# One core, attention followed by a GLU and a bilinear layer: where q and k are split, how v is padded, and who adds a head's two parts

## The chip, the cores and the metric

The kernel runs on one NeuronCore of a Trainium2 chip. A core has five engines that run side by side, each with an in-order queue: TensorE (PE, and PEld for its weight loads), VectorE (DVE), ScalarE (ACT), GpSimd (POOL) and SyncE (SP), which here only issues DMAs. The metric is the device time of one launch in microseconds (us). Three runs of the kernel before took 1189.56 to 1189.74 us, median 1189.6 us.

## The reference

```python
scores = q @ k.T / 8                       # 4 batches x 8 heads, 576 tokens, head_dim 64
scores = where(scores >= scores.max(-1) - tau, scores, -1e9)
attn   = exp(scores - scores.max(-1)); attn /= attn.sum(-1) + 1e-9
x      = (attn @ v)  as [2304 tokens, 512]
x      = (silu(x @ w_gate) * (x @ w_val)) @ w_out        # 512 -> 1536 -> 512
out    = ((x @ w1) * (x @ w2) @ w3) @ w_out2             # 512 -> 1024 -> 512
```

The weights arrive as 64-bit floats and have to be turned into 32-bit ones on the chip.

## The kernel before, in words

Every matmul operand is kept as two parts, `hi` (rounded to the format in which TensorE is fast) and `lo` (what is left), and products are made in three or four passes from these parts.

**Attention.** Work goes by *pairs* of heads, p = 0 to 15, four pairs to a batch. A pair has nine score *tiles* (i = 0 to 8; i = 4 is that of the last 64 queries of both heads, the "left" queries). A tile is scored on TensorE into `s_bank` (`mm_scores`), reduced to its row maximum by VectorE (`el_max`, L482), exponentiated by ScalarE (`el_exp`, L491), masked and summed by VectorE two tiles later (`el_mask`, L501), which needs the threshold that GpSimd adds (`el_thr`, L474, tile `stat`). Two queues of further items are worked off between the tiles by credits (`some`): `main` (transposes of the masked tiles, `it_T` and others, whose `hi` and `lo` go to `AT`, `ATL` through one of three paths X, Y, Z, and the products with v, `it_pv`) and `prep` (the next pair's operands). In path Y the `lo` half is GpSimd's (L100, L103), from a copy of the bank in a `tmp` or `raw` buffer.

`prep` has five items for the next pair: `it_k` and `it_q` transpose k and q into a bank of `t_bank` and copy `hi` out (L340); `it_k2` and `it_q2` subtract `hi` in the bank by a matmul with minus the identity (`less`, L335), copy `lo` out (L345), and issue the twelve DMAs that stack `hi` and `lo` into the operands `L` and `R` (`stack`, L348, L349); `it_left` does the same for the left queries. Prep earns 0.8 credits in a tile.

The v of the last 64 keys has to be padded with zeros to stand in a 128-row operand, `VLZ`. `split_left` splits it for a whole batch into `vls`; `split_v` copies it into `VLZ` for each pair with two DMAs (L309). In the product with v the `hi` part of v gives rows 0 to 63 of `xs` and its `lo` part rows 64 to 127. Both parts are stored separately in DRAM, `x_dram[2, ...]`, with two DMAs for each head (L599).

**GLU and bilinear layer.** The tokens go in five blocks. `x_prep(j, kk)` loads both parts of a piece of x and the reciprocal sums into two 4 KB slots (L790, L795), GpSimd adds the parts (L826), VectorE multiplies (L829), ScalarE and VectorE split the result (L817, L818). Weights are loaded and converted a *unit* at a time: `conv_step` finishes one unit (L157, then L196 on ScalarE and L199 on GpSimd or VectorE) and starts the next (`conv_bits`: L139, L142, L145 on VectorE, L148 and L149 on ScalarE, L150 on GpSimd). The items of `early()` come into `prep` when the last pair starts: three `conv_step` and the four `x_prep` of block 0. Then the GLU begins, `glu_step`, with the matmuls of `mm3` (L835).

The order on each engine is made at build time by a list scheduler that respects the data and the buffers: it may hoist instructions, and what it chose is shown below where it matters.

Of the kernel before, what the change touches and what calls it, by code (L numbers as in the profile page):

```python
# [34 lines left out]
def kernel(  # L35
# [171 lines left out]

    def conv_step(n=1):

        old = []  # L210
        while conv_mid and conv_mid[0][2]() and len(old) < n:
            old.append(conv_mid.popleft())
            old[-1][1](conv_value(old[-1][0]))
# [14 lines left out]
    def attention(actx, early, tail):  # L228
# [8 lines left out]
        ta = lctx.enter_context(tc.tile_pool(name="ta", bufs=N_TA))  # L237
        raw_i, in_tail = [0], []

        def raw_tile():  # L240
            raw_i[0] += 1
            if in_tail or raw_i[0] % (N_TA + N_TMP) >= N_TA:
                return tmp()
            return ta.tile([P, 512], F32, tag="raw", name="raw")

# [105 lines left out]
        halves = {}  # L351

        def it_q(p):
            hi = sp.tile([P, 512], F32R, tag="qhi", name="qhi")
            halves[p, 0] = (turn(raws.pop((p, 0)), hi, 0.125), hi)

        def it_k(p):
            hi = sp.tile([P, 512], F32R, tag="khi", name="khi")
            halves[p, 1] = (turn(raws.pop((p, 1)), hi, 1.0), hi)

        def it_q2(p):
            L, R = qk_tiles(p)
            bank, hi = halves.pop((p, 0))
            lo = sp.tile([P, 512], F32R, tag="qlo", name="qlo")
            turn_lo(bank, hi, lo, 0.125)
            stack(L[:, 0, :], lo, hi, 0)
            stack(L[:, 1, :], hi, lo, 1)
            stack(L[:, 2, :], hi, lo, 0)
            stack(L[:, 3, :], lo, hi, 1)

        def it_k2(p):
            L, R = qk_tiles(p)
            bank, hi = halves.pop((p, 1))
# [759 lines left out]
```

## Time and profile before

| | |
|---|---|
| median of three runs | 1189.6 us |
| the profiled execution | 1189.26 us, of which the span from first to last instruction is 1187.3 us |
| attention, roughly | 0 to 365 us |
| GLU, its weights' conversion included | 358 to 810 us |
| conversion and product of w3 and the second w_out | 810 to 890 us |
| bilinear layer | 890 us to the end |

Busy time is what an engine's instructions cover. TensorE's clock is given as a granted share: 1.00 is 2.4 GHz and 0.50 is 1.2 GHz. A bracket behind a row of the timeline is the idle time before it and what ended that.

### The profile page before, as it was taken

How to read it: one execution, taken by the hardware profiler on the slowest of the kernel's cores; microseconds unless marked ns; L12 is line 12 of the kernel's file. 1: busy time of each engine (PE TensorE's matmuls, PEld its weight loads, DVE VectorE, ACT ScalarE, POOL GpSimd, SP SyncE). 2: the span in 40 equal slices, each digit the busy share in tenths (PEclk: the TensorE clock that was granted, in tenths of full speed). 3: DMA queues.
4: the chain of work that ended last, by engine and by line, in shares of the span. 5: the costliest groups of instructions: out<-in, count | busy, mean ns of one | idle time of the engine just before them, and what ended most of it. 6: DMA issues, size and time to landing. Idle time of an engine off the chain costs nothing.

```text
span 1187.3 us, 16882 instructions
## 1 busy us (share of the span) xinstructions
PE 1122.1 (95%) x6074; PEld 959.8 (81%) x6074; DVE 733.1 (62%) x1272; ACT 590.3 (50%) x1071; POOL 475.7 (40%) x457
## 2 busy tenths in 40 slices
PE   7898998899878999999999999999899999999998
PEld 6788888788766777888888888888787888888886
DVE  7987868778798797656464664567892022432222
ACT  6877878778786456443242432345563231321111
POOL 4575665565663655443232332234241221321110
PEclk9999999999989999999999999999999999999999
DMA  8865756656455743222111120123430010100024
GB/s 197 224 146 141 163 132 142 146 121 142 107 170 167 216 126 100 75 68 71 31 59 36 37 89 8 47 93 103 124 107 18 1 36 1 37 1 1 1 58 102
DMA packets 107891, 108.14 MB, mean 91 GB/s; under 512 B 48800, under 2 KB 82208, under 8 KB 107808
## 3 DMA queue, kind: packets, MB, share of 16 engines
q1 hardware_dynamic: 107808, 107.06, 34.3%
q8 instruction: 48, 0.79, 0.3%
q14 instruction: 35, 0.29, 0.1%
HBM read 68.16 MB, written 14.23 MB: 69 GB/s over the span
## 4 chain that ended last, share of the span: by engine, by line
PE 55%; DVE 5%; DMA 2%; ACT 1%; issue 1%; POOL 0%; POOLq 0%; DVEq 0%; ACTq 0%
PE t_bank L835 36%; PE s_bank L835 19%; DMA raw<-in_moe_w_dram 2%; DVE tmp L157 1%; DVE slot L818 1%; DVE raw L142 1%; DVE tmp L145 1%; DVE tmp L139 0%; DVE slot L911 0%; PE t_bank L908 0%; DVE slot L199 0%; DVE slot L1022 0%; DVE slot L882 0%; DVE slot L1059 0%; ACT raw L148 0%
## 5 line engine op out<-in xcount | busy, mean ns | idle before, releaser
L835 PE MATMUL t_bank<-slot,slot 128*128 128x512 f32 (+1 forms) x2592 | 559.7, 371 | 5.9 <-DVE slot L818 2.4
L835 PEld LDWEIGHTS t_bank<-slot,slot 128*128 128x128 f32 x2592 | 457.0, 189 | 92.8 <-DVE slot L818 3.3
L835 PE MATMUL s_bank<-h,slot 128*128 128x512 f32 (+1 forms) x720 | 161.9, 372 | 3.4 <-ACT slot L884 2.2
L150 POOL TENSOR_TENSOR raw<-raw 128x512 int32<-128x512 int32 x76 | 84.4, 1111 | 182.1 <-ACT raw L149 171.6
L501 DVE SCALAR_TENSOR_TENSOR P<-P,stat,E 128x576 f32<-128x576 f32 x144 | 148.3, 1043 | 5.6 <-POOL stat L474 3.9
L835 PEld LDWEIGHTS s_bank<-h,slot 128*128 128x128 f32 x720 | 126.8, 190 | 27.1 <-ACT slot L884 2.6
L482 DVE TENSOR_SCALAR_CACHE_REDUCE P<-s_bank,neg 128x576 f32<-128x576 f32 x144 | 114.2, 809 | 55.2 <-PE s_bank L443 55.2
L1069 DVE TENSOR_TENSOR tmp<-tmp,t_bank 128x512 f32<-128x512 f32 (+1 forms) x40 | 25.3, 633 | 178.2 <-PE t_bank L835 178.2
L107 POOL TENSOR_TENSOR h<-tmp,h 128x512 fp32r<-128x512 f32 (+1 forms) x60 | 74.4, 1239 | 136.1 <-ACT h L106 136.0
L1073 POOL TENSOR_TENSOR h<-tmp,h 128x512 fp32r<-128x512 f32 (+1 forms) x38 | 45.8, 1205 | 200.5 <-ACT h L1071 200.5
L491 ACT ACTIVATE E<-P,stat 128x576 f32<-128x576 f32 x144 | 116.4, 812 | 9.7 <-DVE P L482 8.8
L443 PE MATMUL s_bank<-R,L 128*128 128x288 f32 x512 | 101.2, 318 | 14.7 <-DVE P L482 5.6
L920 DVE TENSOR_TENSOR tmp<-tmp,t_bank 128x512 f32<-128x512 f32 (+1 forms) x60 | 37.9, 631 | 113.1 <-PE t_bank L835 104.5
L835 PE MATMUL s_bank<-slot,h 128*128 128x512 f32 x432 | 106.6, 391 | 0.9 <-DVE slot L1059 0.8
L328 PE MATMUL t_bank<-ident,P 128*128 128x128 f32 x640 | 90.5, 277 | 14.5 <-DVE AT L524 4.7
L443 PEld LDWEIGHTS s_bank<-R,L 128*128 128x128 f32 x512 | 76.8, 194 | 26.7 <-DVE P L482 15.1
L835 PEld LDWEIGHTS s_bank<-slot,h 128*128 128x128 f32 x432 | 79.9, 188 | 18.3 <-DVE slot L1059 2.1
L882 DVE TENSOR_TENSOR slot<-s_bank,slot 128x1024 f32<-128x1024 f32 (+1 forms) x72 | 82.2, 1146 | 18.5 <-PE s_bank L835 16.5
L328 PEld LDWEIGHTS t_bank<-ident,P 128*128 128x128 f32 x640 | 74.2, 141 | 23.5 <-DVE ATL L524 4.6
L583 PE MATMUL t_bank<-AT,sp 128*128 128x288 f32 x512 | 87.5, 307 | 5.3 <-DVE AT L524 2.4
L157 DVE SCALAR_TENSOR_TENSOR tmp<-tmp,raw 128x512 f32<-128x512 f32 x76 | 72.0, 948 | 30.5 <-POOL raw L150 30.5
L919 ACT ACTIVATE tmp<-t_bank 128x512 f32<-128x512 f32 (+1 forms) x60 | 33.2, 554 | 113.3 <-PE t_bank L835 106.9
(110 smaller groups left out, 1427.9 us busy)
## 6 DMA issues: line engine op xcount, KB each, us to landing
raw<-in_moe_w_dram SPq DMA_DIRECT2D x32, 512.0 KB, 3.8
raw<-in_moe_w_out_dram SPq DMA_DIRECT2D x20, 512.0 KB, 3.5
x_dram<-xs SPq DMA_DIRECT2D x64, 144.0 KB, 2.4
L<-qhi SPq DMA_DIRECT2D x60, 128.0 KB, 2.9
L<-qlo SPq DMA_DIRECT2D x60, 128.0 KB, 2.5
raw<-in_moe_w_gate_dram SPq DMA_DIRECT2D x12, 512.0 KB, 3.7
raw<-in_moe_w_val_dram SPq DMA_DIRECT2D x12, 512.0 KB, 3.8
ld<-in_k_dram SPq DMA_DIRECT2D x16, 256.0 KB, 4.0
```

What stands on the lines that cost most here:

```text
L107: nc.gpsimd.tensor_tensor(out=lo, in0=src, in1=f32(hi), op=ALU.subtract)
L150: nc.gpsimd.tensor_tensor(out=a, in0=a, in1=x, op=ALU.subtract)
L157: nc.vector.scalar_tensor_tensor(out=f32(m), in0=f32(m), scalar=2.0 ** 20, in1=f32(a), op0=ALU.add, op1=ALU.mult)
L328: nc.tensor.matmul(bank[:, t * P:(t + 1) * P], lhsT=part, rhs=ident, is_transpose=True, start=(t == 0), stop=(t == len(parts) - 1),)
L443: nc.tensor.matmul(o, lhsT=lhs, rhs=R[:, c:c + HALF], start=(h == hs2[0] and e == 0), stop=(h == hs2[-1] and e == 1),)
L482: nc.vector.tensor_scalar(out=p_tile(p, i).rearrange("p (a c) -> p a c", a=2), in0=sb[:, :, 0:HALF], scalar1=neg, scalar2=None, op0=ALU.mu ...
L491: nc.scalar.activation(out=e, in_=p_tile(p, i), func=ACTF.Exp, scale=-1.0, bias=stats[p // HP][:, 0, c:c + 1],)
L501: nc.vector.scalar_tensor_tensor(out=t, in0=t, scalar=stats[b][:, 1, c:c + 1], in1=e, op0=ALU.is_le, op1=ALU.mult, accum_out=sums[b][:, c: ...
L583: nc.tensor.matmul(o, lhsT=vs[:, 4 * h + c, :, :].rearrange("p a d -> p (a d)"), rhs=AT[h][:, e, c, cs], start=(c == 0 and e == 0), stop=F ...
L835: nc.tensor.matmul(o, lhsT=lhs(a), rhs=rhs(c), start=(first and i == 0), stop=(last and i == 2))
L882: nc.vector.tensor_tensor(out=a, in0=s, in1=a, op=ALU.add)
L1073: (nc.vector if end else nc.gpsimd).tensor_tensor(out=h[:, 1, 0:n], in0=ab[:, 0:n], in1=f32(h[:, 0, 0:n]), op=ALU.subtract)
```

## The change

Four edits, and some sizes that follow from them.

1. `it_k2` and `it_q2` go. `turn` puts the second half (the matmul with minus the identity, the copy of `lo`, the stacking DMAs) into the list `deferred`, whose entries run behind the next item. Prep has three items for a pair and earns 1.0 credit in a tile.
2. `split_left` writes `VLZ` itself, for all four pairs of a batch, with GpSimd instructions on 64 partitions; two such tiles alternate by batch. The two DMAs of each pair go.
3. Three weight units are converted inside attention, one each in pairs 3, 6 and 9 (from tile 4 on); `early()` only issues loads and the four `x_prep`.
4. GpSimd issues a DMA that adds `xs[64:128]` onto `xs[0:64]`, and SP stores the sum alone. `x_dram` has one part, `x_prep` needs one slot and one load in place of two parts, and GpSimd's addition goes.

The seventh buffer for copies of path Y (`raw`) goes as well, and the slot pools change from 7 and 8 to 6 and 9.

```diff
-N_U1, N_U2, N_U3, N_U4 = 3, 7, 8, 24
-N_TMP, N_BIG, N_HB, N_TA = 6, 3, 3, 1
+N_U1, N_U2, N_U3, N_U4 = 3, 6, 9, 24
+N_TMP, N_BIG, N_HB = 6, 3, 3
+EARLY = (3, 6, 9)
...
+    def conv_end(n=1):
+        old = 0
+        while conv_mid and conv_mid[0][2]() and old < n:
+            bits, done, _ = conv_mid.popleft()
+            done(conv_value(bits))
+            old += 1
+        return old
...
-            vls = wk.tile([P, HP, 2, D], F32R, tag="vls", name="vls", bufs=2)
-            split_pool(vls[:, :, 0, :], vls[:, :, 1, :], vl)
+            for h in range(2):
+                r = slice(64 * h, 64 * h + 64)
+                split_pool(VLZ[b % 2][r, :, h, 0, :], VLZ[b % 2][r, :, h, 1, :], vl[r])
...
-            for h in range(2):
-                r = slice(64 * h, 64 * h + 64)
-                nc.sync.dma_start(out=f32(VLZ[r, p % 2, h]), in_=f32(vls[r, p % HP]))
...
-        def turn(raw, hi, scale):
+        def turn(raw, hi, lo, scale, then):
             bank = t_bank()
             turn_p(bank, [raw[:, t, :, :].rearrange("p h d -> p (h d)") for t in range(4)])
             nc.scalar.activation(out=hi, in_=bank, func=ACTF.Copy, scale=scale)
-            return bank
+            def rest():
+                less(bank, minus_r if scale == 1.0 else minus8_r, hi)
+                nc.scalar.activation(out=lo, in_=bank, func=ACTF.Copy, scale=scale)
+                then()
+            deferred.append(rest)
...
-                for e in range(2):
-                    nc.sync.dma_start(
-                        out=x_dram[e, g * D:(g + 1) * D, b, :], in_=xs[64 * e:64 * e + 64, :]
-                    )
+                nc.gpsimd.dma_start(out=xs[0:64, :], in_=xs[64:P, :], accum_op=ALU.add)
+                nc.sync.dma_start(out=x_dram[g * D:(g + 1) * D, b, :], in_=xs[0:64, :])
...
-            return [lambda f=f: f(p) for f in (it_k, it_q, it_k2, it_q2, it_left)]
+            return [lambda f=f: f(p) for f in (it_k, it_q, it_left)]
...
-            credit[1] += (1.5 if in_tail else 0.8) * frac
+            credit[1] += (1.5 if in_tail else 1.0) * frac
...
-            if n == NS // 2:
-                conv_fetch()
+            if i == 4 and p in EARLY:
+                prep.extend([conv_step, conv_end])
...
-        nc.gpsimd.tensor_tensor(
-            out=xr[:, 0:n], in0=tt[:, 0, 0:n], in1=tt[:, 1, 0:n], op=ALU.add
-        )
-        nc.vector.tensor_tensor(out=xr[:, 0:n], in0=xr[:, 0:n], in1=rg[:, 0, 0:n], op=ALU.mult)
+        nc.vector.tensor_tensor(
+            out=xr[:, 0:n], in0=t[:, 0, 0:n], in1=t[:, 1, 0:n], op=ALU.mult
+        )
...
-        r = [conv_step] * 3
-        for kk in range(KD):
-            r.insert(2 * kk + 1, lambda kk=kk: x_prep(0, kk))
-        return r
+        conv_fetch()
+        return x_items(0)
```

Over the whole program the two orders differ in these counts: 32 DMAs of `xs<-xs` are new on GpSimd, its 20 additions of L826 go, and its eight instructions for `vls` become sixteen, half as tall, for `VLZ`; SP loses the 32 DMAs to `VLZ` and 32 of its 64 stores to `x_dram`. TensorE, ScalarE and VectorE have as many instructions of each kind as before.

On VectorE, the last pair (its tiles are `P`, the maxima are L482 and the masks L501), before:

```order
L139 TENSOR_SCALAR tmp<-raw 128x512 x3
L482 TENSOR_SCALAR P,stat<-s_bank,neg 128x576
L142 TENSOR_SCALAR raw<-raw 128x512
L145 SCALAR_TENSOR_TENSOR tmp<-raw,tmp 128x512
L482 TENSOR_SCALAR P,stat<-s_bank,neg 128x576
L829 TENSOR_TENSOR tmp<-tmp,slot_4543 128x512
L142 TENSOR_SCALAR raw<-raw 128x512
L145 SCALAR_TENSOR_TENSOR tmp<-raw,tmp 128x512
L501 SCALAR_TENSOR_TENSOR P,sums<-P,stat,E 128x576
```

and the same place in the changed kernel, where `tmp<-slot` (L819) is the multiplication of block 0 that was L829:

```order
L480 TENSOR_SCALAR P,stat<-s_bank,neg 128x576 x2
L499 SCALAR_TENSOR_TENSOR P,sums<-P,stat,E 128x576 x2
L521 TENSOR_TENSOR AT<-t_bank,AT 128x512
L480 TENSOR_SCALAR P,stat<-s_bank,neg 128x576 x2
L819 TENSOR_TENSOR tmp<-slot_4535 128x512
L819 TENSOR_TENSOR tmp<-slot_4556 128x512
L499 SCALAR_TENSOR_TENSOR P,sums<-P,stat,E 128x576
```

The conversions of three units are gone from between the maxima and the masks; the multiplications stand two tiles later.

One of these units in the changed kernel, on VectorE at the border of pairs 3 and 4 (L141, L144, L147, L159 are the old L139, L142, L145, L157; `r<-sums` belongs to the end of a batch):

```order
L499 SCALAR_TENSOR_TENSOR P,sums<-P,stat,E 128x576
L141 TENSOR_SCALAR tmp<-raw 128x512
L601 TENSOR_SCALAR r<-sums 128x36
L144 TENSOR_SCALAR raw<-raw 128x512
L147 SCALAR_TENSOR_TENSOR tmp<-raw,tmp 128x512
L604 RECIPROCAL r<-r 128x36
L521 TENSOR_TENSOR AT<-t_bank,AT 128x512
L480 TENSOR_SCALAR P,stat<-s_bank,neg 128x576 x2
L159 SCALAR_TENSOR_TENSOR tmp<-tmp,raw 128x512
```

Three of its four instructions stand behind the last mask of one pair and ahead of the first maximum of the next.

On GpSimd around the product with v of pair 0, in the changed kernel (`sp` is the split v of a later pair, `stat` the thresholds, `AT` the lower halves of path Y):

```order
L105 TENSOR_TENSOR AT<-tmp,AT 128x512
L595 DMA xs<-xs 64x576
L472 TENSOR_SCALAR stat<-stat,tau_sb 128x2
L102 TENSOR_SCALAR sp_919<-ld_343 128x8x64
L105 TENSOR_TENSOR sp_919<-ld_343,sp_919 128x8x64
L595 DMA xs<-xs 64x576
L472 TENSOR_SCALAR stat<-stat,tau_sb 128x2
L102 TENSOR_SCALAR AT<-tmp 128x512
L105 TENSOR_TENSOR AT<-tmp,AT 128x512
```

where before there was:

```order
L103 TENSOR_TENSOR AT<-tmp,AT 128x512
L474 TENSOR_SCALAR stat<-stat,tau_sb 128x2
L100 TENSOR_SCALAR sp_923<-ld_345 128x8x64
L103 TENSOR_TENSOR sp_923<-ld_345,sp_923 128x8x64
L474 TENSOR_SCALAR stat<-stat,tau_sb 128x2
L100 TENSOR_SCALAR AT<-tmp 128x512
L103 TENSOR_TENSOR AT<-tmp,AT 128x512
```

A DMA stands on either side of the split of v, in each pair, and a threshold is queued behind each of them.

## Rows read from the trace of the kernel before

**Rows 1.** The page: busy us (share of the span) x instructions.
```profile
PE 1122.1 (95%) x6074; PEld 959.8 (81%) x6074; DVE 733.1 (62%) x1272; ACT 590.3 (50%) x1071; POOL 475.7 (40%) x457
```

**Rows 2.** Attention: windows of 20 us, summed; and the group of maxima, 20 to 330 us.
```profile
sum 300.00, PE 270.33 PEld 244.63 DVE 247.32 ACT 244.90 POOL 181.79; mean PE 18.02 PEld 16.31 DVE 16.49 ACT 16.33 POOL 12.12
...
L482 DVE TENSOR_SCALAR_CACHE_REDUCE P<-s_bank,neg 128x576 f32<-128x576 f32 x133 | 105.4, 809 | 50.1 <-PE s_bank L443 50.1
```

**Rows 3.** Waits, 20 to 330 us: total us, times, longest us.
```profile
DVE P L482 <- PE s_bank L443: 50.1, 15, 6.3
...
POOL sp L100 <- PE t_bank L583: 43.9, 10, 6.5
...
DVE P L501 <- POOL stat L474: 3.9, 8, 1.2
...
PE s_bank L443 <- DMA L<-qlo: 2.1, 4, 1.3
```

**Rows 4.** Windows: us, busy of each engine, granted clock, DMA share, GB/s.
```profile
104.00:108.00 4.00, 3.88 (x17) 3.57 (x17) 2.03 (x5) 1.02 (x3) 0.10 (x1) 0.57 0.12 25
...
330.00:360.00 30.00, 21.67 (x129) 18.48 (x128) 30.00 (x55) 24.36 (x45) 18.42 (x15) 0.89 0.59 172
...
340.00:348.00 8.00, 5.54 (x27) 5.44 (x28) 8.00 (x16) 6.56 (x11) 4.49 (x4) 0.57 0.13 39
...
360.00:460.00 100.00, 89.66 (x437) 72.88 (x436) 84.07 (x109) 55.50 (x95) 53.83 (x42) 0.98 0.57 161
```

**Rows 5.** VectorE groups, 330 to 365 us: busy us, mean ns, idle before.
```profile
L157 DVE SCALAR_TENSOR_TENSOR tmp<-tmp,raw 128x512 f32<-128x512 f32 x3 | 4.2, 1411 | 0.0
...
L145 DVE SCALAR_TENSOR_TENSOR tmp<-raw,tmp 128x512 f32<-128x512 uint16 x4 | 3.1, 782 | 0.0
...
L142 DVE TENSOR_SCALAR raw<-raw 128x512 int32<-128x512 int32 x4 | 2.8, 712 | 0.0
...
L199 DVE TENSOR_TENSOR slot<-tmp,slot 128x512 fp32r<-128x512 f32 x1 | 1.7, 1749 | 0.0
...
L139 DVE TENSOR_SCALAR tmp<-raw 128x512 int32<-128x512 int32 x4 | 1.6, 445 | 0.0
```

**Rows 6.** Timeline of TensorE, 338 to 343 us: start us, us, instruction, idle before.
```profile
338.47 0.66 PE L328 MATMUL t_bank<-ident,P 128*128 128x128 f32 x4 [2.34 <-ACT AT L518]
...
342.46 0.90 PE L328 MATMUL t_bank<-ident,P 128*128 128x128 f32 x3 [3.33 <-DVE ATL L524]
```

**Rows 7.** Groups of L829, L818 (365 to 460 us), L826 (325 to 460 us); one L829.
```profile
L829 DVE TENSOR_TENSOR tmp<-tmp,slot 128x512 f32<-128x512 f32 (+1 forms) x16 | 18.5, 1159 | 5.9 <-POOL tmp L826 4.7 <-DMA slot<-r_dram 1.2
...
L818 DVE TENSOR_TENSOR slot<-tmp,slot 128x512 fp32r<-128x512 f32 (+1 forms) x16 | 13.4, 842 | 1.0 <-ACT slot L817 0.8
...
L826 POOL TENSOR_TENSOR tmp<-slot 128x512 f32<-128x512 f32 (+1 forms) x20 | 27.5, 1379 | 9.5 <-DMA slot<-x_dram 6.5 <-DVE slot L818 2.7 <-DMA slot<-r_dram 0.2
...
373.71 0.68 DVE L829 TENSOR_TENSOR tmp<-tmp,slot 128x512 f32<-128x512 f32 x1
```

**Rows 8.** DMA issues: count, KB each, median us to landing.
```profile
x_dram<-xs SPq DMA_DIRECT2D x64, 144.0 KB, 2.4
...
slot<-x_dram SPq DMA_DIRECT2D x8, 512.0 KB, 6.1
```

**Rows 9.** Timeline of one pair, 150 to 169 us.
```profile
150.76 1.18 SPq L599 DMA_DIRECT2D x_dram<-xs  x2
...
153.33 0.80 ACT L595 COPY xs<-t_bank 128x288 f32<-128x288 f32 x2 [0.80 <-PE t_bank L588]
...
154.14 0.62 POOL L100 TENSOR_SCALAR sp<-ld 128x512 fp32r<-128x512 f32 x1
...
154.44 0.82 DVE L482 TENSOR_SCALAR_CACHE_REDUCE P<-s_bank,neg 128x576 f32<-128x576 f32 x1 [5.01 <-PE s_bank L443]
...
157.43 1.16 POOL L100 TENSOR_SCALAR AT<-raw 128x512 fp32r<-128x512 f32 x1
...
168.44 1.30 PE L583 MATMUL t_bank<-AT,sp 128*128 128x288 f32 x8
```

More of the change, by code (lines that the diff above doesn't have):

```diff
@@ L77 @@
     ps = ctx.enter_context(tc.tile_pool(name="ps", bufs=1, space=PSUM))
-    x_dram = dram.tile([2, DM, B, S], F32, name="x_dram")
+    x_dram = dram.tile([DM, B, S], F32, name="x_dram")
     r_dram = dram.tile([B, H, S], F32, name="r_dram")
@@ L206, in conv_fetch @@
             conv_raw.append((conv_load(src), *rest))
+    def conv_end(n=1):
[5 more added lines that the diff above has]
+        return old
     def conv_step(n=1):
[L210 to L213, printed above, removed]
+        old = conv_end(n)
         new = 0
@@ L236, in attention @@
         sp = lctx.enter_context(tc.tile_pool(name="sp", bufs=1))
[L237 to L244, printed above, removed]
+        in_tail = []
         ATT = at.tile([P, 2, 2, 4, S], F32R, name="AT")
@@ L251, in attention @@
         nc.gpsimd.memset(f32(LZ), 0.0)
-        VLZ = at.tile([P, 2, 2, 2, D], F32R, name="VLZ")
-        nc.gpsimd.memset(f32(VLZ), 0.0)
+        VLZ = [at.tile([P, HP, 2, 2, D], F32R, name=f"VLZ{n}") for n in range(2)]
+        for t in VLZ:
+            nc.gpsimd.memset(f32(t), 0.0)
         raws, lraw, splits, lsplit, lrs = {}, {}, {}, {}, {}
@@ L349, in stack, with then @@
             nc.sync.dma_start(out=f32(dst[64:P, :]), in_=f32(bottom[64 * h:64 * h + 64, :]))
-        halves = {}
         def it_q(p):
+            L, R = qk_tiles(p)
             hi = sp.tile([P, 512], F32R, tag="qhi", name="qhi")
-            halves[p, 0] = (turn(raws.pop((p, 0)), hi, 0.125), hi)
+            lo = sp.tile([P, 512], F32R, tag="qlo", name="qlo")
+            def then():
+                stack(L[:, 0, :], lo, hi, 0)
+                stack(L[:, 1, :], hi, lo, 1)
+                stack(L[:, 2, :], hi, lo, 0)
+                stack(L[:, 3, :], lo, hi, 1)
+            turn(raws.pop((p, 0)), hi, lo, 0.125, then)
         def it_k(p):
+            L, R = qk_tiles(p)
             hi = sp.tile([P, 512], F32R, tag="khi", name="khi")
[L359 to L373, printed above, removed]
             lo = sp.tile([P, 512], F32R, tag="klo", name="klo")
-            turn_lo(bank, hi, lo, 1.0)
-            stack(R[:, 0:512], hi, lo, 0)
-            stack(R[:, 640:1152], lo, hi, 1)
+            def then():
+                stack(R[:, 0:512], hi, lo, 0)
+                stack(R[:, 640:1152], lo, hi, 1)
+            turn(raws.pop((p, 1)), hi, lo, 1.0, then)
         def turn_r(parts, dst):
@@ L528, in evac_split @@
             else:
-                raw = raw_tile()
+                raw = tmp()
                 rv = raw
@@ L786, in x_load @@
         c0, n = blocks[j]
-        x_raw[j, kk] = [take(F32) for _ in range(2)]
-        tt, rg = x_raw[j, kk]
+        t = x_raw[j, kk] = take(F32)
         for o, b, c, m in segs(c0, n):
             nc.sync.dma_start(
-                out=tt[:, :, o:o + m],
-                in_=x_dram[:, kk * P:(kk + 1) * P, b, c:c + m].rearrange("e p c -> p e c"),
+                out=t[:, 0, o:o + m], in_=x_dram[kk * P:(kk + 1) * P, b, c:c + m]
             )
```

20 lines of the change are left out of this document (8 added, 12 removed).

## The prediction, made before the changed kernel ran

> **What bounds the kernel now.** I began with the page. TensorE is busy for 1122 of 1187 us [rows 1], and the change takes no instruction from it, so all there is to win is its 65 us of idle time, and what it works at the lower clock. Where these lie, the windows say. In attention, 20 to 320 us, it is busy for 270.3 of 300 us [rows 2]: 29.7 us idle, 3.0 us in each 30 us, with VectorE at 247 us and GpSimd at 182 us. So TensorE is the bound there, and the others have room. In the last pair, 330 to 360 us, VectorE is busy for 30.0 of 30.0 us and TensorE for 21.7 [rows 4]: VectorE is the bound, and TensorE idles 8.3 us, 5.4 us more than elsewhere in attention. From 360 to 460 us TensorE idles 10.3 us, VectorE works 84 of 100. From there to the end I found nothing that the change touches.
>
> Next I read what ends the idle times. In the last pair TensorE waits 2.34 us for a copy of ScalarE and soon after 3.33 us for a subtraction that is queued on VectorE [rows 6]; behind that, from 340 to 348 us, the granted clock is 0.57 [rows 4], close to the lower level of 1.2 GHz, and of its 5.54 busy us about 0.43 x 5.54 = 2.4 us are lost to it. In attention proper the waits are small and of many kinds; one that the change aims at is TensorE waiting for the DMAs that build `L`, 2.1 us in four cases [rows 3], and behind the longest of them, 104 to 108 us, the clock is 0.57 too [rows 4]: 0.43 x 3.88 = 1.7 us. Last I looked at where VectorE and GpSimd have their gaps. VectorE waits 50.1 us for scores, 15 times [rows 3], once for each pair: it is the time in which TensorE multiplies with v. GpSimd's split of v waits 43.9 us for the same products to end [rows 3].
>
> **Part 1: three units out of the last pair.** There VectorE spends on them: L157 4.2 us for three, L145 3.1, L142 2.8 and L139 1.6 us for four each, so three quarters of them, and L199 once, 1.7 us [rows 5]. That is 4.2 + 2.3 + 2.1 + 1.2 + 1.7 = 11.5 us taken from the engine that is the bound. TensorE can get back no more than its 5.4 us above the usual idle and the 2.4 us of low clock, 7.8 us in all; after that it is the bound itself. I take 6.5, since the four `x_prep` stay and their loads now come later. Bounds: 2 (only the 2.34 us wait shrinks, the maxima still wait in line) and 7.8.
>
> **Part 2: GpSimd's additions go from `x_prep`.** 20 of 1.379 us, 27.5 us [rows 7]; four of them in the last pair, 16 behind it. They hang on to VectorE as well: L829 takes 1.159 us in the mean from 365 to 460 us, and 0.68 us where nothing runs beside it; L818 0.842 us [rows 7]. 16 x (1.159 - 0.68) + 16 x (0.842 - 0.68) = 10.3 us of VectorE's 84 are such stretching, most of it against GpSimd's work, of which the additions are the largest group. The load of a block is halved as well (512 KB, 6.1 us to landing, [rows 8]). I take 2 us of TensorE's 10.3 us idle, bounds 0 (other conversions stretch VectorE as before) and 6.
>
> **Part 3: the same three units inside attention.** By the sum above a unit is 11.5 / 3 = 3.8 us of VectorE, in pairs that last 310 / 133 x 9 = 21 us [rows 2]. The order puts three of the four VectorE instructions into the gap behind the last mask of a pair, which is 50.1 / 15 = 3.3 us long; that gap is the cover. What does not fit delays the first maxima of the next pair. I take 0.3 us a unit, 1 us; bounds 0 and 11.5 (no cover at all).
>
> **Part 4: q and k.** Same matmuls, copies and DMAs. The stacking of q comes with the second item at 1.0 credits a tile, so about tile 2, where it came with the fourth at 0.8, about tile 5. The operands are needed two tiles before the pair ends, so the waits for `L` should go: 2.1 us and the 1.7 us of low clock. Other waits will take some of it: I take 2.5 us, bounds 0 and 3.8. A new wait is the one for the copy of `hi` one item later; it is hidden by that item's own matmuls, about a microsecond.
>
> **Part 5: v padded by GpSimd, fewer DMAs.** Four batches with two instructions more, each on half the partitions: nothing for TensorE, hidden by the third of its time that GpSimd has free. On SP 32 DMAs to `VLZ` and 32 stores go, 0.59 us each to issue [rows 9]; SP is waited for in nothing but `L`, counted above. The seventh copy buffer goes; six remain for at most three copies in flight, so 0.
>
> **Part 6: the DMA on GpSimd.** The trace has no DMA that GpSimd issues, so its price is bounded from rows. Below: what SP takes to issue a store of the same bytes, 0.59 us (1.18 us for two, [rows 9]). Above: GpSimd is held until the transfer has landed, 2.4 us as the store of these bytes takes [rows 8]. Between these I take what one GpSimd instruction over such a tile takes, 1.4 us [rows 7], the row it is nearest to: it, too, stands in GpSimd's queue as one instruction. Two for a pair are 2.8 us; GpSimd is idle for (300 - 182) / 300 x 21 = 8.3 us of a pair. The first is free: it may go as soon as the first head's copy is there, when GpSimd would wait for the second head's products anyway. The second waits for the last copy, which began at 153.33 us and ended at 154.13, just when GpSimd took up the split of v (154.14) [rows 9]. Queued behind it are thresholds and the lower halves of path Y. A mask needs its threshold two tiles on, 4.7 us; the lower half begun at 157.43 us is read by the products that begin at 168.44 [rows 9], 11 us later. That is the cover. If it were gone, each of 15 pairs would pay 1.4 us. I take 0.1 us a pair, 1.5 us; bounds 0 and 15 x 2.4 = 36 us. On SP the store now waits for the addition, and the stacking of `R` and `L` waits behind the store: 2.4 us late, against three tiles (7 us) won in part 4.
>
> The Trainium skill, "SBUF — State Buffer", section "SBUF: two separate sides", speaks against this part: descriptors of a DMA that GpSimd issues are written by GpSimd's own cores, and these are locked out of the port that they share with VectorE while certain VectorE instructions run; its example goes from 620 to about 3100 ns. By that figure, as an estimate, the 32 DMAs would hold GpSimd for 99 us, 6.2 us in each pair, and put the sum on the side of rival A. No row here shows such a DMA.
>
> **The sum.** -6.5 - 2 + 1 - 2.5 + 0 + 1.5 = -8.5 us. Against the profiled execution's 1189.26 us that is 1180.8; this execution is 0.3 us under the median of the three runs, so I say **1181 us**. A difference under 0.2% (2.4 us) could hardly be told from no change.
>
> **Rivals.**
> *A, GpSimd's queue becomes the bound in each pair (slower).* The DMA does not fall into the gap but runs beside VectorE's masks, and each holds the other up as L829 shows (1.159 for 0.68 us). A DMA that lasts d makes a pair longer once two of them exceed the 8.3 us that GpSimd has free, or once a threshold comes more than 4.7 us late, which is the nearer point: d above 2.3 us. Say each of 15 pairs then pays 1.2 us, 18 us in all, of which the 8.5 us won are taken off: 1199 us. For it: masks already wait for thresholds 3.9 us in 8 cases [rows 3]. Against: 8.3 us free in a pair, and the DMAs stand where VectorE is idle. The skill's rule above, in the same section, would bring this about if the lock is met often. Chance 0.2.
> *B, what the last pair gains is given back (no change).* The loads of x for block 0 come later, through two slots in turn; VectorE stands in line at L819 for them. The third load can go only when the first multiplication has freed its slot, and such a load takes up to 6.1 us [rows 8], while seven VectorE instructions stand between, 5.7 us at the 0.81 us of a maximum [rows 2]. If each of two turns costs 2 us and the units in attention 3 us, the sum is -8.5 + 4 + 2 = -2.5, and with parts 2 and 4 at half, about 0: 1189 us. Chance 0.17.
> *C, more than I sum.* Parts 1, 2 and 4 at their best ends, -7.8 - 6 - 3.8, with 1 + 1.5 to pay: -15, 1174 us. Chance 0.13.
> The forecast itself, 1177 to 1186 us, has 0.45. The remaining 0.05 goes to a new order on TensorE that happens to fit worse, 1192 us.
>
> **The numbers.** Faster by over 0.2%: the forecast, C and 0.02 of B, 0.60. Within 0.2%: 0.14 of B. Slower: A, the worse order and the rest of B, 0.26. The range has to reach C at 1174 and into A, whose lower half lies from 1192 to 1198; 1174 to 1196 leaves out about 2 in 10. The forecast's own range is 1177 to 1186.
>
> **What would show it.** In the last pair VectorE no longer full, TensorE's idle time in those 30 us near 3 us, and no clock of 0.57 behind it. In pairs 3, 6 and 9 the units inside VectorE's gap, which shrinks there. No wait of TensorE for `L<-qlo`. GpSimd's DMAs well under 2.3 us, and VectorE's wait for `stat` near 3.9 us in total. L829's successor nearer to 0.68 us. I am wrong if VectorE's wait for `stat` grows to tens of us, if TensorE idles at the head of a pair for `AT` from GpSimd, or if L819 waits for `x_dram` in the last pair.

## The result, and the profile of the changed kernel

The changed kernel took 1195.5 us in the median of six runs (1191.0 to 1198.4), the kernel before 1189.6 in the runs beside it (1185.9 to 1191.5). The ratio is 1.0054, 95% interval 1.0032 to 1.0076: slower by half a per cent, where I had said 1181 us. Its profiled execution has a span of 1190.7 us against 1187.3.

The page, its rows of busy time [rows 1] and of the new DMA (count, KB, median us to landing):

```profile
PE 1122.6 (94%) x6074; PEld 961.9 (81%) x6074; DVE 718.0 (60%) x1272; ACT 591.5 (50%) x1071; POOL 472.8 (40%) x478
...
xs<-xs POOLq DMA_DIRECT2D x32, 144.0 KB, 3.2
```

The windows that answer to [rows 2, 4]: attention, then the last pair, then the stretch up to 460 us.

```profile
sum 300.00, PE 261.75 PEld 236.55 DVE 250.76 ACT 242.22 POOL 196.85; mean PE 87.25 PEld 78.85 DVE 83.59 ACT 80.74 POOL 65.62
...
330.00:360.00 30.00, 25.38 (x158) 23.10 (x159) 27.08 (x57) 21.80 (x42) 13.15 (x16) 0.89 0.51 128
360.00:460.00 100.00, 93.05 (x458) 77.64 (x457) 63.81 (x101) 56.06 (x97) 35.12 (x28) 0.95 0.47 128
```

From 330 to 460 us the forecast came in part: VectorE is no longer full in the last pair, and TensorE idles 11.6 us there (30 - 25.4 and 100 - 93.05) where it idled 18.7. But more goes to its clock: at 0.89 and 0.95 that is 0.11 x 25.4 + 0.05 x 93.05 = 7.4 us, against 0.11 x 21.7 + 0.02 x 89.7 = 4.2 us before [rows 4]; so some 3 of the 7.1 us are spent again. The rest is lost ahead of that, and more. In the 300 us of attention TensorE is busy for 261.8 us in place of 270.3, 8.6 us more idle time. The waits there, 20 to 330 us (total us, times, longest), show new names [rows 3]:

```profile
PE s_bank L441 <- DMA L<-qlo: 9.8, 9, 2.0
...
PE s_bank L441 <- DMA L<-qhi: 1.8, 1, 1.8
...
DVE P L499 <- POOL stat L472: 10.6, 19, 1.5
...
SPq L596 <- DMA xs<-xs: 77.0, 21, 9.1
```

TensorE's wait for `L`, which was to go, rose from 2.1 to 11.6 us. SP stands for 77 us at the store of `x_dram`, which waits for GpSimd's addition; what is queued behind it stands as well. Standing is not new to SP: before, it stood about as long at the copies into `VLZ` (L309), which this change takes away. The two largest of those waits, in the kernel before:

```profile
SPq L309 <- PE t_bank L588: 27.8, 9, 5.2
SPq L309 <- PE t_bank L328: 19.6, 10, 2.9
```

One pair's start in the timeline of the changed kernel, SP first, then TensorE:

```profile
140.79 0.47 SPq L596 DMA_DIRECT2D x_dram<-xs  x1
141.35 0.66 SPq L282 DMA_DIRECT2D ld<-in_q_dram  x1
142.10 0.77 SPq L350 DMA_DIRECT2D R<-khi  x1
142.92 1.50 SPq L351 DMA_DIRECT2D R<-khi  x1
...
145.82 0.70 SPq L351 DMA_DIRECT2D R<-klo  x1
146.56 0.60 SPq L350 DMA_DIRECT2D R<-klo  x1
147.27 0.54 SPq L350 DMA_DIRECT2D L<-qlo  x1
...
150.61 0.60 SPq L351 DMA_DIRECT2D L<-qhi  x1
...
141.00 0.47 PE L334 MATMUL t_bank<-khi,minus_r 128*128 128x512 f32 x1
142.65 0.40 PE L334 MATMUL t_bank<-qhi,minus_r 128*128 128x512 f32 x1
149.86 0.50 PE L441 MATMUL s_bank<-R,L 128*128 128x288 f32 x2 [2.00 <-DMA L<-qlo]
```

The second halves of k and q (L334) run 1.65 us apart. SP needs about 0.6 us for each of the twelve stacking DMAs (one took 1.50), and their row lasts from 142.1 to 151.2 us; R's are still being issued 4.5 us after the start of q's product, and the first scores of the pair wait 2.00 us for `L`.

### The profile page after: what moved, and what is told of

Its sections match the earlier page's. It is cut to its first block, busy times and chain, and to the rows that moved or that the text cites. A ratio compares the mean times of both kernels' runs of the same rounds, so it can differ in the third digit from the quotient of the medians.

```text
span 1190.7 us, 16845 instructions
## 1 busy us (share of the span) xinstructions
PE 1122.6 (94%) x6074; PEld 961.9 (81%) x6074; DVE 718.0 (60%) x1272; ACT 591.5 (50%) x1071; POOL 472.8 (40%) x478
## 4 chain that ended last, share of the span: by engine, by line
PE 70%; DVE 12%; DMA 6%; ACT 4%; POOL 3%; issue 3%; SPq 1%; ACTq 0%; POOLq 0%; DVEq 0%
PE t_bank L827 38%; PE s_bank L827 20%; PE t_bank L580 4%; DVE P L499 4%; PE s_bank L441 3%; DVE P L480 3%; PE t_bank L327 2%; DMA raw<-in_moe_w_dram 2%; ACT E L489 1%; DMA L<-qlo 1%; DVE tmp L159 1%; PE t_bank L585 1%; DVE slot L811 1%; DMA raw<-in_moe_w_gate_dram 1%; DMA x_dram<-xs 1%
## 5 line engine op out<-in xcount | busy, mean ns | idle before, releaser
L109 POOL TENSOR_TENSOR h<-tmp,h 128x512 fp32r<-128x512 f32 (+1 forms) x60 | 76.8, 1280 | 149.4 <-ACT h L108 149.4
L1059 DVE TENSOR_TENSOR tmp<-tmp,t_bank 128x512 f32<-128x512 f32 (+1 forms) x40 | 25.4, 634 | 178.2 <-PE t_bank L827 178.2
L1063 POOL TENSOR_TENSOR h<-tmp,h 128x512 fp32r<-128x512 f32 (+1 forms) x38 | 45.8, 1205 | 200.5 <-ACT h L1061 200.5
L327 PE MATMUL t_bank<-ident,P 128*128 128x128 f32 x640 | 95.5, 283 | 9.6 <-DVE ATL L564 3.2
L159 DVE SCALAR_TENSOR_TENSOR tmp<-tmp,raw 128x512 f32<-128x512 f32 x76 | 69.9, 920 | 37.2 <-POOL raw L152 37.2
L150 ACT ACTIVATE raw<-raw,ebias 128x512 int32<-128x512 int32 x76 | 57.9, 763 | 61.0 <-DVE tmp L147 47.6
```

The costliest lines, as they stand in the source:

```text
L109: nc.gpsimd.tensor_tensor(out=lo, in0=src, in1=f32(hi), op=ALU.subtract)
L150: nc.scalar.activation(out=a, in_=x, func=ACTF.Relu, scale=8.0, bias=ebias[:, 0:1])
L159: nc.vector.scalar_tensor_tensor(out=f32(m), in0=f32(m), scalar=2.0 ** 20, in1=f32(a), op0=ALU.add, op1=ALU.mult)
L327: nc.tensor.matmul(bank[:, t * P:(t + 1) * P], lhsT=part, rhs=ident, is_transpose=True, start=(t == 0), stop=(t == len(parts) - 1),)
```

## Experiments

Times are medians; each stands against runs of the kernel before beside it.

| run | us | before | ratio, 95% interval |
|---|---|---|---|
| e1, no accumulation | 1199.9 | 1189.4 | 1.0093 (1.0075 to 1.0111) |
| e2, store doesn't wait | 1195.8 | 1189.4 | 1.0062 (1.0043 to 1.0081) |
| e3, before + accumulation | 1200.5 | 1189.4 | 1.0091 (1.0074 to 1.0109) |
| e4, units late | 1200.1 | 1189.4 | 1.0091 (1.0070 to 1.0112) |
| e5, before + halves | 1200.9 | 1188.4 | 1.0113 (1.0084 to 1.0143) |
| e6, before + VLZ | 1188.0 | 1188.4 | 1.0001 (0.9989 to 1.0013) |
| e7, before + early units | 1185.5 | 1188.4 | 0.9971 (0.9961 to 0.9980) |
| n1, before, two items swapped | 1188.8 | 1188.4 | 1.0008 (0.9997 to 1.0018) |
| e8, changed, no halves | 1194.7 | 1188.9 | 1.0057 (1.0035 to 1.0078) |
| e9, VLZ + early units | 1186.5 | 1188.9 | 0.9978 (0.9965 to 0.9991) |
| h1, e5 with R by ScalarE | 1224.5 | 1188.9 | 1.0298 (1.0267 to 1.0328) |
| h2, e5 spaced | 1185.0 | 1188.9 | 0.9974 (0.9958 to 0.9989) |
| f1, e8, store doesn't wait | 1184.0 | 1188.8 | 0.9964 (0.9947 to 0.9980) |
| f2, all but accumulation, spaced | 1183.2 | 1188.8 | 0.9947 (0.9928 to 0.9966) |
| f3, changed, spaced | 1184.8 | 1188.8 | 0.9968 (0.9954 to 0.9982) |
| f4, before's places | 1189.0 | 1188.8 | 0.9998 (0.9983 to 1.0013) |
| g1, e5 at credit 0.8 | 1190.9 | 1187.8 | 1.0026 (1.0013 to 1.0040) |
| g2, e5, last queries fifth | 1200.4 | 1187.8 | 1.0099 (1.0080 to 1.0118) |

### First theory: SP's store alone (e1 to e4)

e1 puts the two stores and GpSimd's addition back into the changed kernel:

```diff
-nc.gpsimd.dma_start(out=xs[0:64, :], in_=xs[64:P, :], accum_op=ALU.add)
-nc.sync.dma_start(out=x_dram[g * D:(g + 1) * D, b, :], in_=xs[0:64, :])
+for e in range(2):
+    nc.sync.dma_start(out=x_dram[e, g * D:(g + 1) * D, b, :], in_=xs[64 * e:64 * e + 64, :])
```

> The change without its accumulating DMA: SP stores both parts of a head as before, GpSimd adds them in x_prep; the deferred halves, the early units and GpSimd's VLZ stay. Theory S (SP's store waits for the accumulation, and the stacks of R and L queued behind it come late): the waits of SP's store for xs (83 us) go, TensorE's wait for L (11.3 us up to 345 us) falls to 2 to 4 us, and the time is 1183 to 1187 us, under the kernel before. Rival U (the early units in pairs 3, 6 and 9 cost it): no gain from this edit, 1193 to 1197. Rival V (GpSimd's splits of VLZ and its late thresholds cost it): the same, 1193 to 1197.

e2 changes one operand of the store:

```diff
-nc.sync.dma_start(out=x_dram[g * D:(g + 1) * D, b, :], in_=xs[0:64, :])
+nc.sync.dma_start(out=x_dram[g * D:(g + 1) * D, b, :], in_=xs[64:P, :])
```

> The changed kernel with its accumulating DMA kept, but the store takes the upper 64 partitions of xs, which the accumulation only reads; so the output lacks the sum of the two parts, and the store waits for ScalarE's copy alone. Theory S: SP's wait at the store falls from 83 us to under 20, TensorE's wait for L to 2 to 4 us, time 1184 to 1188. A second form of it, G (the accumulation's cost lies in GpSimd's queue, not in SP's): no gain, 1193 to 1197, with the store's wait gone and VectorE still waiting 10 us for GpSimd's thresholds. Rivals U and V: 1193 to 1197 too, with TensorE's wait for L still at 9 us or more.

e3 is the reverse of e1, made in the kernel before. e4 takes the early units back:

```diff
-EARLY = (3, 6, 9)
+EARLY = ()
...
-        conv_fetch()
-        return x_items(0)
+        r = [conv_step] * 3
+        for kk in range(KD):
+            r.insert(2 * kk + 1, lambda kk=kk: x_prep(0, kk))
+        return r
```

> The kernel before with the accumulating DMA, the single store and the shorter loading of x, and nothing else of the change. Theory S: SP's store waits 60 to 90 us for the accumulation, the L wait of TensorE rises from 2 us, and 5 to 8 us are lost ahead of 330 us, of which 2 to 3 come back where GpSimd no longer adds x: 1191 to 1196 us. Rivals U and V: within 1186 to 1189, since neither the early units nor GpSimd's VLZ are in it.

> The changed kernel with its three early units back in the last pair, among the pieces of x as before. Theory S: the wait of SP's store stays at about 80 us and TensorE's for L at about 10; the last pair takes its 3 to 6 us back, the pairs lose 0 to 2: 1195 to 1200 us. Rival U: the 8.8 us more of idle TensorE between 20 and 330 us go, 1188 to 1191.

Measured: e1 1199.9, e2 1195.8, e3 1200.5, e4 1200.1 us. My theory fell in this form: without the accumulation the kernel was not faster but 4.4 us slower, and with a store that doesn't wait for it no different. e1's wait of TensorE for `L` stayed at 9.2 us, so something else makes `L` late. Neither run took SP's standing away, though: the store now waits as long for ScalarE's copy. SP, 20 to 330 us, in e1 and then e2:

```profile
SPq L596 <- ACT xs L592: 87.7, 20, 9.2
...
SPq L596 <- ACT xs L592: 89.1, 21, 7.4
```

Rival U fell with e4. But e3 said that the accumulation by itself costs 11 us in the kernel before, more than theory S allowed, and with little of it in TensorE's wait for `L`:

```profile
PE s_bank L443 <- DMA L<-qlo: 3.6, 5, 1.2
```

So at least two causes, and not additive ones.

### One part at a time (e5 to e7, n1)

Each puts one part into the kernel before: e5 `turn` with its `deferred` second half, three items and the credit of 1.0; e6 `VLZ`, with the room it takes; e7 the early units. n1 changes only an order:

```diff
-            r = [lambda: it_kl(p), lambda: it_corner(p)]
+            r = [lambda: it_corner(p), lambda: it_kl(p)]
```

> The kernel before with the deferred second halves of q and k alone (three items of a pair and the credit of 1.0 with it). Theory L (the second halves come later, so L's last stacks do): TensorE's wait for L rises from 2.1 to 9 us or more between 20 and 330 us, 2 to 5 more falls of the granted clock at 1.6 us each, 1194 to 1202 us. Rival O (any other order of the same work loses the few pauses that the order of before happens to have): also slower, 1192 to 1200, but with the pauses spread over other waits as well and not mainly L's. If neither, 1187 to 1190.

> The kernel before with VLZ written by GpSimd alone, and what its room needs: no seventh raw buffer, one slot moved from the second pool to the third. Theory L: no part in it, 1186 to 1191, the wait for L at 1 to 4 us. Rival V (GpSimd's work and the lost buffer): VectorE's wait for thresholds rises from 3.9 to 10 us, 1193 to 1197. Rival O: 1192 to 1200, two or more further falls of the clock, at waits of several kinds.

> The kernel before with the three early units in pairs 3, 6 and 9 alone. Theory L: the last pair is relieved as forecast by 3 to 6 us, the pairs pay 1 to 2: 1184 to 1188. Rival U (units in the attention cost more than they save): 1192 to 1197, with SP's raw loads waiting 20 us for VectorE. Rival O: 1190 to 1200, with more falls of the clock though the last pair has less to do.

> The kernel before with two neighbouring items of each pair swapped, the corner's transposes ahead of the last keys' ones: no instruction, byte or buffer more or less. Theories L, U and V: within 0.2% of before, 1187 to 1192. Rival O: slower by 2 to 8 us, 1191 to 1198, as every other order that was run, with one to five further falls of the granted clock at about 1.6 us each.

Measured: halves +12.6 us, `VLZ` -0.4, early units -2.9, the swap +0.5. So rival O falls (the swap costs nothing that can be told from zero), U and V fall, and theory L stands, though without the further falls of the clock that it expected (2.8 us lost to the clock from 20 to 330 us in e5, 3.3 before, summed as in the last section). TensorE's wait for `L` in e5, 20 to 330 us, against 2.1 us before [rows 3]:

```profile
PE s_bank L444 <- DMA L<-qlo: 14.1, 10, 2.7
```

e6 warns against pricing such rows one by one. SP stands at its store there, TensorE waits for `L` longer than theory L allowed (4 us), and its time is that of the kernel before:

```profile
SPq L589 <- ACT xs L585: 62.1, 23, 4.1
...
PE s_bank L433 <- DMA L<-qlo: 6.8, 7, 2.3
```

### Why the halves cost so much (h1, h2, f4, g1, g2)

```diff
h1: stack(R[:, 0:512], hi, lo, 0)  ->  the same by nc.scalar.dma_start, and R's other two
h2: (it_k, it_q, it_left), credit 1.0  ->  (it_k, pause, it_q, pause, it_left), credit 0.8
f4: (it_k, it_q, it_left), credit 1.0  ->  (it_k, it_q, pause, pause, it_left), credit 0.8
g1: credit 1.0  ->  0.8
g2: (it_k, it_q, it_left)  ->  (it_k, it_q, pause, pause, it_left)
```

> The kernel before with the deferred halves alone (1200.9 us), but R's four stacks of each pair are issued on ScalarE's queue and only L's eight on SP's. Theory B (k's and q's stacks now come close together, and twelve issues of 0.6 us in a row on SP make L's last ones late): SP's row is 2.4 us shorter, TensorE's wait for L falls from 14.1 us to 6 or less, 1191 to 1196. Rival D (it is the place of q's second half among the scores that is too late, not SP's row): the wait for L stays above 10, 1198 to 1203.

> The kernel before with the deferred halves, the credit at 0.8 as before, and two empty items so that k comes first, q third and the last queries and keys fifth, 2.5 tiles apart: each second half still goes behind the next item. Theory B: R's stacks are issued well ahead of L's, the wait for L is 2 to 6 us, 1187 to 1193. Rival F (a deferred half is itself late, whatever the spacing): the wait for L above 10 us, 1198 to 1203.

> The kernel before with the deferred halves at credit 0.8 and five items, two of them empty, but k and q first and second and the empty ones behind them: it differs from the spaced run (1185.0 us) in their order alone. Theory B (distance of k and q): TensorE's wait for L is 8 us or more again, 1193 to 1202. Rival K (it was the credit, and the place of the last queries and keys): 1184 to 1189, the wait for L under 4 us.

> The kernel before with the three items k, q, last queries and keys, at the old credit of 0.8. Theory Z (the last queries and keys are prepared at the third item, where LZ is still to be read by the pair under way; their transposes hold a bank until then, and k and q behind other work come late beside the scores): slow, 1194 to 1202 us, with TensorE's wait for L at 8 us or more. Theory K (the credit of 1.0 alone does it): 1186 to 1190.

> The kernel before with k and q first and second at credit 1.0, two empty items, and the last queries and keys fifth. Theory Z: about as the kernel before, 1186 to 1191, TensorE's wait for L under 4 us. Theory K: 1194 to 1202, the wait for L at 8 us or more. If both runs lie between 1190 and 1195, credit and place share the cost.

h2 took 1185.0 us, 16 us less than e5 and 2 below theory B's range, with the same deferral; its wait for `L` is 2.3 us, 20 to 330 us. f4 told nothing of the distance: it came out with the instructions of the kernel before in the same order on all five engines, and with its time. That is a finding too: deferring a half "behind the next item" is no change in itself; only the places of the items are. g1 (1190.9) and g2 (1200.4) then separate these: the credit of 1.0 costs nearly all, the place of the last queries and keys some 3 us at the credit of 0.8 and hardly anything at 1.0 (g2 against e5). So theory Z fell, and K held, though g1 lies 0.9 us above its range. h1 was meant to shorten SP's row and made things worse (below), so it decides nothing.

What goes with the time is the distance from k's second product to q's. From the timelines, the median over 14 pair starts: 3.9 to 4.0 us in the kernel before, f4 and g1; 1.5 to 1.7 in e5 and g2; 2.2 in the changed kernel; 6.8 in h2 and 7.7 in f3. Where it is about 4, R's last stacking DMA has just been issued when q's product begins, and L's last has been issued 5.2 to 5.5 us after that. Where it is 1.5 to 2.2, R's are still being issued for 2.5 to 3 us and L's last is out 6.6 to 7.1 us after q's product began, with the scores due. h2's timeline at a like place, SP and then TensorE:

```profile
114.55 0.55 SPq L353 DMA_DIRECT2D R<-khi  x1
...
117.72 0.84 SPq L353 DMA_DIRECT2D R<-klo  x1
...
120.60 0.46 SPq L354 DMA_DIRECT2D L<-qhi  x1
...
125.17 0.59 SPq L353 DMA_DIRECT2D L<-qlo  x1
...
114.94 0.40 PE L335 MATMUL t_bank<-khi,minus_r 128*128 128x512 f32 x1
...
120.72 0.40 PE L335 MATMUL t_bank<-qhi,minus_r 128*128 128x512 f32 x1
128.75 0.50 PE L444 MATMUL s_bank<-R,L 128*128 128x288 f32 x2
```

R's are all issued before q's product runs, L's last is issued 3 us ahead of the scores, and they don't wait. g2's waits, 20 to 330 us, are those of e5 again:

```profile
PE s_bank L444 <- DMA L<-qlo: 14.4, 9, 2.7
...
PE s_bank L444 <- DMA L<-qhi: 5.0, 2, 2.8
```

### The accumulation once more (e8, e9, f1 to f3)

e8 is the changed kernel with the items and the credit of before, e9 the same with two stores and GpSimd's addition. f1 is e8 with e2's edit, f3 the changed kernel with h2's items and credit, and f2 is f3 with e1's edit.

> The changed kernel with the second halves of q and k as items of their own again (five items, credit 0.8); GpSimd's VLZ, the early units and the accumulating DMA stay. Theory L (the halves are what costs it, since they alone cost the kernel before 12.6 us): TensorE's wait for L falls from 9.8 us to 6 or less between 20 and 330 us, and the time to 1182 to 1187. Rival S2 (the accumulating DMA costs about 11 us in every company, as it did alone): 1193 to 1198, with no gain over the changed kernel.

> GpSimd's VLZ and the early units without the halves and without the accumulating DMA (two stores, and GpSimd adds the parts of x). Theory L: the two parts add up as they were alone, 0 and -2.9 us: 1184 to 1187. Theory S2: the same here, so that the run before this one would be some 10 us slower than this; by theory L the two are within 4 us.

> The run without halves (accumulating DMA, early units, GpSimd's VLZ; 1194.7 us) with the store taking the upper 64 partitions of xs, which the accumulation only reads: the output lacks the sum of the two parts, GpSimd's 32 DMAs stay, and SP's store no longer waits for them. Theory S (the accumulation costs by SP's wait, since the loads of k and q and R's stacks stand behind the store): SP's wait at the store falls from 96 to about 55 us, TensorE's wait for L to 2 to 3 us, 1185 to 1189 us. Rival G (the cost lies in GpSimd's queue): no gain, 1193 to 1197.

> Deferred halves with k and q spaced by empty items, GpSimd's VLZ and the early units, with two stores and no accumulating DMA. If the gains found apart add up (halves spaced -3.9, VLZ and early units -2.4 us): 1181 to 1184, the fastest so far. If they overlap, because each only fills the same idle time of TensorE: 1184 to 1187.

> The changed kernel with nothing else than k and q spaced (two empty items, credit 0.8). Theory B (k and q close together are what makes the halves costly, and the accumulation adds its own): TensorE's wait for L falls from 9.8 us to 5 or less, the time to 1187 to 1193, between the run before this one and the changed kernel. If spacing does not help here: 1194 to 1198.

Measured: e8 1194.7, e9 1186.5, so here the accumulation costs 8 us. In e8 theory L's wait came (5.1 us), its time did not: that is rival S2's. f1, which keeps all of GpSimd's 32 DMAs and no longer waits for them at the store, took 1184.0, 10.7 us less: by the whole time theory S holds, and rival G as it was put down falls. SP's largest wait and TensorE's for `L`, 20 to 330 us, in e8:

```profile
SPq L596 <- DMA xs<-xs: 95.7, 23, 9.4
...
PE s_bank L440 <- DMA L<-qlo: 5.1, 6, 1.7
```

and in f1:

```profile
SPq L596 <- ACT xs L592: 59.0, 17, 6.2
...
PE s_bank L440 <- DMA L<-qlo: 3.4, 6, 1.1
```

The way is not the one that theory S named. With all releasers counted SP stands at the store for 102 us in e8 and for 87 in f1, and the wait for `L` is only 1.7 us shorter. The windows of e8 and then f1:

```profile
20.00:330.00 310.00, 270.64 (x1932) 243.87 (x1933) 263.02 (x583) 252.28 (x505) 207.84 (x243) 0.99 0.65 145
330.00:460.00 130.00, 117.07 (x625) 99.49 (x624) 90.61 (x157) 76.17 (x137) 43.68 (x40) 0.96 0.45 124
```

```profile
20.00:330.00 310.00, 274.40 (x1938) 247.27 (x1937) 263.12 (x584) 251.91 (x506) 208.65 (x242) 0.98 0.64 144
330.00:460.00 130.00, 122.69 (x661) 105.05 (x661) 96.64 (x167) 81.35 (x147) 50.22 (x45) 0.97 0.48 132
```

TensorE is busy for 3.8 us more in f1's pairs, but at 0.98 in place of 0.99 some 3 us of that are the slower clock, and the pairs are not over sooner. The first maximum of the last pair, in e9, e8 and f1:

```profile
327.17 0.82 DVE L479 TENSOR_SCALAR_CACHE_REDUCE P<-s_bank,neg 128x576 f32<-128x576 f32 x1 [3.23 <-PE s_bank L440]
...
336.71 0.82 DVE L479 TENSOR_SCALAR_CACHE_REDUCE P<-s_bank,neg 128x576 f32<-128x576 f32 x1 [3.10 <-PE s_bank L440]
...
338.64 0.82 DVE L479 TENSOR_SCALAR_CACHE_REDUCE P<-s_bank,neg 128x576 f32<-128x576 f32 x1 [3.09 <-PE s_bank L440]
```

So in these profiles the accumulation costs the pairs 10 us with the wait and 11 us without it, and all that f1 gains on e8 lies behind them: it is 1.9 us late at the last pair and 7.3 us early at the end (1181.7 against 1189.0). Up to 330 us the two have the same order on TensorE but for a few instructions, so this is no matter of order. From 330 to 460 us SP's store waited another 23.7 us for the addition in e8, 13.1 us of it at once, and 12.6 us for ScalarE in f1. Queued behind it are the loads of x and of the next weights. The last store of x and VectorE's wait for those weights, in e8 and then f1:

```profile
384.81 0.46 SPq L596 DMA_DIRECT2D x_dram<-xs  x1
398.70 0.43 DVE L141 TENSOR_SCALAR tmp<-raw 128x512 int32<-128x512 int32 x1 [3.55 <-DMA raw<-in_moe_w_gate_dram]
...
378.51 0.46 SPq L596 DMA_DIRECT2D x_dram<-xs  x1
392.74 0.83 DVE L141 TENSOR_SCALAR tmp<-raw 128x512 int32<-128x512 int32 x1 [0.60 <-DMA raw<-in_moe_w_gate_dram]
```

What the accumulation costs the pairs is open. TensorE waits there longer for VectorE's maxima (9.1 us in e9, 19.2 in e8, 16.9 in f1), and VectorE's masks take longer; 20 to 330 us, in e9, e8 and f1:

```profile
L498 DVE SCALAR_TENSOR_TENSOR P<-P,stat,E 128x576 f32<-128x576 f32 x133 | 134.3, 1024 | 3.3 <-POOL stat L471 2.2 <-ACT E L488 1.1
...
L498 DVE SCALAR_TENSOR_TENSOR P<-P,stat,E 128x576 f32<-128x576 f32 x130 | 137.6, 1074 | 2.4 <-POOL stat L471 2.3
...
L498 DVE SCALAR_TENSOR_TENSOR P<-P,stat,E 128x576 f32<-128x576 f32 x130 | 138.4, 1080 | 2.4 <-POOL stat L471 2.3
```

130 x 0.05 is 6.5 us. It would fit that GpSimd's other work, moved by two DMAs a pair, meets more masks; so for the pairs rival G stands, and no run tests it.

f3, the changed kernel with nothing but two empty items and the old credit, took 1184.8 us: 10.7 less than the changed kernel, 4 less than the one before and 2 below its range. TensorE's wait for `L` is 0.7 us up to 345 us. With k and q spaced the accumulation costs at most little: f2, without it, took 1183.2 us, and the two intervals overlap. f2 is the fastest version that computes everything, 0.53% under the kernel before.

## Why the prediction was wrong

- **Part 4 is the step that failed first.** I priced it at -2.5 us with bounds 0 and 3.8 of gain, since "the stacking of q comes with the second item at 1.0 credits a tile, so about tile 2, where it came with the fourth at 0.8, about tile 5". That was read from the credits, not from the compiled order. In the order of TensorE q's first products stand behind six of the pair's nine score tiles in both kernels (median from the third pair on); what moved is k, from behind three to behind five, close to q. The mechanism, operands stacked by SP in time, was the right one; the sign was not: alone the part costs 12.6 us (e5), and in this kernel spacing k and q gives 10.7 us back, with the wait for `L` gone from 11.6 to 0.7 us (f3). A gain of the size forecast, 3.9 us, is there when k is spaced ahead of q (h2), but not on the way forecast: the wait for `L` is 2.3 us there and was 2.1 before. Where it comes from is open.
- **Part 6, the sentence on SP, is the second.** "2.4 us late, against three tiles (7 us) won in part 4" set its cost on SP at 0. The 7 us were never won, and the store's wait for the addition costs 10.7 us (e8 against f1); but the wait for `L` is only 1.7 us of that, and in the profiles the time comes back at the start of the GLU, not in the pairs. Which transfer behind the store makes it late there was not tested. GpSimd's own share was priced at 1.5 us and is not settled: f1 as a whole is 2.5 us under e9, with overlapping intervals, but its pairs are 11 us longer, and what follows is as much shorter, where GpSimd's additions and half of x's loads are gone (part 2).
- **The sum.** With `VLZ` and the early units in the kernel, neither of parts 4 and 6 gives 1186.5 us (e9), part 6 alone 1194.7 (e8), part 4 alone 1199.9 (e1), both 1195.5. Each by itself brings the loss, and the second adds nothing to it: so to take back part 4 alone, or part 6 alone, wins nothing. That both delay the row of stackings on SP explains at most part of this, since the wait for `L` is small where part 6 is alone (4.5 us in e3, 5.1 in e8); why they don't add is not shown. Nor is the cause of e1's 4.4 us above the changed kernel, whose intervals just touch. Its TensorE idles 3.3 us more from 330 to 460 us (115.17 busy against 118.43), which would fit part 2; no run tests that.
- **Parts 1 and 3** were forecast at -6.5 and +1: -2.9 us alone (e7), -4.6 in the changed kernel (e4 against it). Right in mechanism, too large in size; in the last pair the clock of 0.89 [rows 4] stayed.
- **Part 2** was not run alone. The stretching that it was priced by did go: L819, the old L829, takes 0.79 us in the mean in place of 1.16 [rows 7].

```profile
L819 DVE TENSOR_TENSOR tmp<-slot 128x512 f32<-128x512 f32 (+1 forms) x15 | 11.6, 793 | 7.2 <-DMA slot<-x_dram 4.2 <-DMA slot<-r_dram 2.3 <-issue 0.3
```

- **Part 5** at 0 was right: -0.4 us (e6).
- **Rivals.** A's price for a DMA on GpSimd, above 2.3 us, did not come: it holds GpSimd for 0.85 us. VectorE's wait for thresholds did grow, to 10.6 us, but that goes with the halves: it is 12.5 us in e5, where no such DMA is, and 2.3 in e8, where they all are. That masks get longer, as A said, is seen in e8 and f1, and is no matter of the DMA itself: the five masks of e8 that run beside such a DMA alone take 0.81 us, as do the 38 beside which GpSimd is idle. B did not happen. The "new order on TensorE that happens to fit worse", to which I gave 0.05, is half of what decided, and it was no chance matter but a row of DMAs with a due time.

Open besides: why the item scheme at credit 1.0 ends in a compiled order with k behind five score tiles. The runs show that it does, and what it costs.

## What to carry to other kernels

When items move, count in the compiled order of the waiting engine, between the producer and its deadline, and then count what the issuing queue must send in that time: here twelve DMAs at about 0.6 us, which came in time when k led q by 4 us and did not at 2. A wait on a queue is priced by what stands behind it in that queue, also in stages far from the edit: SP's 62 us at a store cost nothing in e6, while in e8 the store's wait cost 10.7 us, which came back only behind the pairs. Look where in the span the time comes back before naming the way. And parts need not add: undo them in pairs, not only one by one.

## What the runs showed of the hardware

A DMA that GpSimd issues to add 64x576 values within SBUF takes 0.85 us of GpSimd and 3.2 us to landing (medians of 32 in the changed kernel); here are two of f1, the first with VectorE idle, the second beside a maximum and a subtraction of VectorE:

```profile
131.63 0.86 POOL L595 DMA_DIRECT2D xs<-xs  x1 [0.57 <-ACT xs L592]
135.92 0.84 POOL L595 DMA_DIRECT2D xs<-xs  x1
```

The Trainium skill, "SBUF — State Buffer", section "SBUF: two separate sides", gives 620 ns for a DMA issued by GpSimd, which become about 3100 beside certain VectorE work. In the changed kernel all 32 hold GpSimd for 0.80 to 1.14 us and land after 2.8 to 4.6, so this case doesn't show it. Fifteen of them run beside a mask, and none of these holds GpSimd for more than 0.99 us.

Two issuing queues were no relief. With R's stackings on ScalarE's queue (h1) ScalarE spent 0.5 us on each, but L's own came to land in 4.4 and 4.0 us (from `qhi` and `qlo`), where e5 has 2.8 and 2.5, and the time rose by 23.5 us. The Trainium skill, "DMA: Bandwidth & Descriptors", section "Issuing engines are not separate DMA queues", says that such a spread saves issue time only, since all share the same DMA engines. That there is no gain agrees; the loss goes beyond it, and its cause is not tested.

A pause of TensorE can cost more than itself. Ahead of 150 us TensorE was busy for 5.33 of 8 us in the changed kernel and last waited the 2.00 us shown above; behind that the granted clock falls, for part of the stretch, from 1.00 to the lower of its two levels, 1.2 GHz:

```profile
142.00:150.00 8.00, 5.33 (x38) 4.25 (x37) 8.00 (x20) 8.00 (x18) 7.36 (x9) 1.00 0.85 187
150.00:156.00 6.00, 4.97 (x26) 4.66 (x27) 5.57 (x12) 2.27 (x5) 2.50 (x3) 0.72 0.59 129
```

(1 - 0.72) x 4.97 is 1.4 us. Summed in this way over windows of 2 us, the kernel before loses 8.9 us to the clock, the changed one 12.6, f4 with the order of before 5.0. So most waits for `L` were not followed by such a fall: from 20 to 330 us both kernels lose about as much to the clock (3.3 and 3.1 us). f4's span is 1183.0 us where before's is 1187.3: one profiled execution differs from another of the same order by 4.3 us, more than the 3.4 us between the profiles before and after the change. So times are compared by medians here, and what is read from single profiles carries that scatter.
